# A memory-augmented attention kernel: the V projection of two steps in five passes, with the columns laid out by step pairs

## The chip, the cores and the metric

One NeuronCore of a Trainium2 chip. The metric is the device time of one execution in microseconds (us); lower is better. Each kernel was run a few times on the chip beside the kernel before. A run agrees with the next to about 0.3%.

## The reference, cut to what matters

The model has two layers. Each is an attention that walks over 64 segments of 32 tokens, carrying 8 memory rows from one segment to the next, followed by a gated feed-forward block. The width is 576, with 32 heads of 128 and a feed-forward width of 4608.

```python
for s in range(n_seg):                                  # 64 segments, strictly in order
    h = concatenate([mem, x[:, s*32:(s+1)*32]], axis=1)  # 8 memory rows + 32 tokens
    q, k, v = h @ Wq, h @ Wk, h @ Wv                     # 40 x 576 by 576 x (32 heads x 128)
    p = softmax(where(mask, q @ k.T * scale, -1e9))
    o = (p @ v) @ Wo
    mem = o[:, :8]                                       # the next segment needs this
    outs.append(o[:, 8:])
...
x = x + attention(layernorm(x)); x = x + silu_ffn(layernorm(x))   # twice
```

## The kernel before

The kernel runs 71 steps. In a step, layer 0 works on segment t and layer 1 on segment t − 7 (the constant `LAG`), so in 57 steps both layers are at work and their 40 columns share each matmul as 80 columns.

The order of TensorE's work is a fixed string of letters: a first part, a block of four steps repeated 11 times, and a last part. The letters that matter here are Q/q for the Q and K projections, S for scores, T for the transposes of the probabilities, P for probabilities times V, O/o for the output projection and its 64-row tail, X/x and V/v for the V projection of token and memory rows, F and W for the feed-forward block, and a, b, n, p for small transposes. "a" and "b" transpose the layer-normed rows of layer 0 and layer 1, four segments (a group) at a time; from there the rows are copied into `HT`, the transposed input of the projections. A small planner inside the kernel, with a cost for every instruction, decides in which order ScalarE and VectorE do the rest. Each engine then works through its own queue in that order.

The V projection of before takes three passes in a two-layer step: two for the token rows (two strips of 32 tokens for each of two quarters of the heads) and one for the memory rows, whose strip holds only 16 columns.

```python
POOLS = {"bank": 7, "y": 1, "qkt": 4, "vx": 2, "vm": 1, ..., "w2": 3, "htt": 4}

def v_mm(self, t, b, strips, tail):          # one pass: 4 column strips side by side
    for c in ((4,) if tail else range(4)):
        for r in (0, 1):
            for p0, c0, c1, q in strips:
                ...                          # 512 columns of Wv per matmul

def vx(self, t, k, b, tail):                 # tokens: k = 0, 1, so two passes
    todo = [(32*(2*ab + li), li, 2*k + ab) for ab in (0, 1) for li in (0, 1)]   # two layers
    ...
def vm(self, t, b, tail):                    # memory of both layers: one pass, 16 columns a strip
    return lambda n: self.v_mm(t, b, [(64*ab + 32*k, SEG, SEG + 2*MEM, 2*k + ab) ...], tail)
```

The layer norm's write into `HT` is one entry in one engine's queue for a whole group. Steps that lie side by side in `HT` are merged, so that it comes to 3 or 6 copies:

```python
def ln_nodes(tag, src, xn, deps, prio, wr, cost, wdeps):
    ...                                                   # stats, power, scaling on DVE and POOL
    d = node("PE", 5*0.056, em.ln_tr(xn, b[0]), ...)      # transposes into one PSUM bank
    return node("AD", cost, wr(b[0]), deps=[d], ...)      # one entry, on ScalarE or VectorE

def ht_write(self, li, g, b):
    ...                                                   # runs of neighbouring steps are merged
    for j0, s0, m in runs:
        self.cp(n, HT[:, s0:s0+m, 0:4, co:co+SEG], ps[:, 0:4, ...])     # m steps in one copy
        for r in (0, R64):
            self.cp(n, HT[r:r+R64, s0:s0+m, 4, co:co+SEG], ps[R64:P, 4, ...])
```

## Time and profile before

| | before |
|---|---|
| time, median of 3 | 2851.08 us (2850.7 to 2856.34) |
| TensorE busy | 98%, 62221 matmuls |
| VectorE, ScalarE, GpSimd busy | 75%, 38%, 2% |
| one block of four steps | 166.2 us |
| V projection | 7960 matmuls, 199 passes |

In the profile PE is TensorE, ACT is ScalarE, DVE is VectorE and POOL is GpSimd; L521 is a line of the kernel. All matmuls are issued from one helper line, all ScalarE copies from a second and all VectorE instructions from a third (L521, L524 and L527 here; L539, L542 and L545 in the changed kernel), so groups are told apart by the tiles they write and read. The prediction shows the page's lines.

### The profile page before, as it was taken

What the parts mean: (1) busy time and instruction counts of PE and PEld (TensorE: products, weight loads), DVE (VectorE), ACT (ScalarE), POOL (GpSimd) and SP (SyncE); (2) the same over time, 40 slices, a digit from 0 to 9 for tenths busy, and PEclk for the clock granted to TensorE, in tenths of its full rate; (3) what the DMA queues carried; (4) which work ended last, traced back from release to release, by engine and by line L of the source; (5) the groups of instructions that cost most, each with busy time, mean ns of one, the idle gap of its engine ahead of it and who ended that gap; (6) DMA issues with size and microseconds to landing.
All of it is one profiled execution on the core that took longest, in us unless ns stands there. A gap on an engine that the chain in (4) does not pass through costs nothing.

```text
span 2847.9 us, 137052 instructions
## 1 busy us (share of the span) xinstructions
PE 2784.7 (98%) x62221; PEld 2269.2 (80%) x62221; DVE 2129.7 (75%) x5300; ACT 1076.2 (38%) x2808; POOL 58.8 (2%) x110
## 2 busy tenths in 40 slices
PE   4999999999999999999999999999999999999998
PEld 3787887888888878888887888888788888788886
DVE  3677777777777787777778777777877777777776
ACT  1444343433434343343434334343333434343332
POOL 1000000000000000000000000000000000000000
PEclk9999999999999999999999999999999999999998
DMA  9063524234242433424243342424334242434467
GB/s 308 6 178 90 163 59 131 84 100 138 65 124 65 137 88 99 137 65 126 65 138 88 97 138 67 123 66 138 88 97 137 68 124 59 138 94 117 128 182 235
DMA packets 493416, 323.85 MB, mean 114 GB/s; under 512 B 26680, under 2 KB 488000, under 8 KB 492832
## 3 DMA queue, kind: packets, MB, share of 16 engines
q1 hardware_dynamic: 489808, 308.15, 36.9%
q8 instruction: 486, 7.96, 1.1%
q0 software_dynamic: 3024, 6.93, 0.8%
q14 instruction: 98, 0.80, 0.1%
HBM read 310.26 MB, written 2.36 MB: 110 GB/s over the span
## 4 chain that ended last, share of the span: by engine, by line
PE 92%; issue 4%; DMA 1%; DVE 1%; ACT 1%; SPq 0%; POOL 0%; DVEq 0%; ACTq 0%; POOLq 0%
PE bank L521 80%; PE YB L521 13%; DMA W<-in_A_Wk_dram 1%; DMA WV<-in_A_Wv_dram 0%; DVE HTT L527 0%; ACT HT L524 0%; DVE STAT L527 0%; DMA W2C<-in_B_w_dram 0%; DVE SME L527 0%; SPq L530 0%; DVE XR L527 0%; DVE QKT L527 0%; DVE PB L527 0%; ACT PTS L524 0%; DVE OT L527 0%
## 5 line engine op out<-in xcount | busy, mean ns | idle before, releaser
L521 PEld LDWEIGHTS <-W 128*128 128x128 bf16 (+1 forms) x29040 | 1212.5, 98 | 142.3 <-issue 56.4
L521 PE MATMUL bank<-HT,W 128*128 128x80 bf16 (+3 forms) x22720 | 821.5, 197 | 10.2 <-issue 5.7
L521 PE MATMUL bank<-XTB,W 128*128 128x256 bf16 (+3 forms) x6320 | 659.5, 262 | 0.1
L521 PE MATMUL bank<-WV,HT 128*32 128x512 bf16 (+3 forms) x7960 | 449.5, 382 | 18.6 <-DMA WV<-in_A_Wv_dram 18.2
L524 ACT ACTIVATE QKT<-bank 128x320 bf16<-128x320 f32 (+1 forms) x714 | 262.2, 409 | 487.0 <-PE bank L521 459.4
L521 PE MATMUL YB<-OT,WO 128*128 128x80 bf16 (+3 forms) x11360 | 434.8, 199 | 7.1 <-ACT HT L524 4.4
L521 PEld LDWEIGHTS <-WO 128*128 128x128 bf16 (+1 forms) x11400 | 389.7, 102 | 58.2 <-issue 43.7
L521 PEld LDWEIGHTS <-HT 128*32 128x32 bf16 (+3 forms) x7960 | 171.0, 92 | 215.6 <-issue 61.2
L527 DVE TENSOR_TENSOR PB<-SME,STAT 40x256 bf16<-40x256 f32 (+1 forms) x1024 | 321.4, 318 | 16.7
L521 PE MATMUL bank<-W2C,HTT 128*128 128x288 bf16 x2232 | 315.5, 287 | 1.8 <-DVE HTT L527 1.0
L527 DVE CAST QKT<-bank 128x320 bf16<-128x320 f32 (+1 forms) x422 | 183.8, 455 | 169.9 <-PE bank L521 167.4
L527 DVE TENSOR_REDUCE STAT<-SME 104x8 f32<-104x320 f32 (+1 forms) x568 | 272.4, 480 | 49.4 <-ACT SME L524 41.7
L527 DVE SCALAR_TENSOR_TENSOR XR<-bank,XR 128x288 f32<-128x288 f32 x576 | 247.3, 450 | 35.4 <-PE bank L521 23.8
L524 ACT ACTIVATE HTT<-bank 128x512 bf16<-128x512 f32 (+1 forms) x324 | 177.5, 549 | 237.6 <-PE bank L521 236.9
L521 PEld LDWEIGHTS <-HTT 128*128 128x128 bf16 x2304 | 209.1, 98 | 64.3 <-issue 11.0
L524 ACT ACTIVATE PTS<-bank 128x320 bf16<-128x320 f32 (+1 forms) x395 | 149.5, 408 | 208.0 <-PE bank L521 182.9
L527 DVE SCALAR_TENSOR_TENSOR HTT<-HTT,bank 128x512 bf16<-128x512 bf16 (+1 forms) x324 | 202.1, 624 | 33.1 <-ACT HTT L524 31.0
L524 ACT ACTIVATE SME<-SME 104x320 f32<-104x320 f32 (+1 forms) x284 | 133.1, 469 | 237.6 <-DVE SME L527 236.1
L527 DVE TENSOR_TENSOR HTT<-HTT,bank 128x512 bf16<-128x512 bf16 (+1 forms) x324 | 203.5, 628 | 22.1 <-PE bank L521 0.9
L524 ACT ACTIVATE OT<-bank 128x320 bf16<-128x320 f32 (+1 forms) x364 | 140.5, 406 | 185.1 <-PE bank L521 183.3
L527 DVE TENSOR_TENSOR SME<-bank,maskb 104x320 f32<-104x320 f32 (+1 forms) x284 | 137.4, 488 | 61.8 <-PE bank L521 57.9
L527 DVE CAST OT<-bank 128x320 bf16<-128x320 f32 (+1 forms) x204 | 94.3, 463 | 80.2 <-PE bank L521 77.3
(69 smaller groups left out, 1850.8 us busy)
## 6 DMA issues: line engine op xcount, KB each, us to landing
W<-in_B_w_dram SPq DMA_DIRECT2D x612, 256.0 KB, 3.5
W2C<-in_B_w_dram SPq DMA_DIRECT2D x306, 288.0 KB, 3.1
W<-in_B_w_dram SPq DMA_DIRECT2D x612, 32.0 KB, 3.0
W<-in_B_w_dram SPq DMA_DIRECT2D x10, 512.0 KB, 8.1
XR<-in_A_x_dram POOLq DMA_DIRECT2D x16, 288.0 KB, 2.8
WO<-in_A_Wo_dram SPq DMA_DIRECT2D x4, 1152.0 KB, 11.2
W<-in_A_Wq_dram SPq DMA_DIRECT2D x8, 512.0 KB, 8.2
W<-in_A_Wk_dram SPq DMA_DIRECT2D x8, 512.0 KB, 7.9
```

The costliest lines, as they stand in the source:

```text
L521: self.ch("PE", self.nc.tensor.matmul(out, lhsT=lhsT, rhs=rhs, start=start, stop=stop, skip_group_check=True, **k))
L524: self.ch("ACT", self.nc.scalar.activation(*a, **k))
L527: self.ch("DVE", getattr(self.nc.vector, fn_)(*a, **k))
```

## The change

Steps are taken in pairs. The second step of a pair leaves 16 of its 64 token rows out of the token passes, and they travel in the strips of its memory rows. Of a pair's 6 passes, 5 are left: two for tokens, one for the memory of the first step, two for the second step's memory with the 16 token rows. For that, `HT` is laid out as pairs of 160 columns, and the columns of the two layers are split and interleaved differently in the two steps. It follows that

- the copy out of the Q/K banks becomes two copies (256 and 64 columns),
- the write of a layer-norm group becomes four separate entries, one per step, each free to go to ScalarE or VectorE: 12 copies for layer 0 and, because layer 1's columns are split in two pieces, 24 for layer 1,
- the probabilities need zeros in new places, which GpSimd sets,
- the weight buffers of the second feed-forward matrix go from 3 to 2, and the V buffers become one pool of 4,
- the order string was searched anew.

```diff
-POOLS = {... "vx": 2, "vm": 1, ... "w2": 3, ...}
+POOLS = {... "v": 4, ... "w2": 2, ...}
+def role(t):
+    return (t - LAG) % 2

-        d = node("PE", 5 * 0.056, em.ln_tr(xn, b[0]), deps=[c] + list(wdeps), ...)
-        return node("AD", cost, wr(b[0]), deps=[d], prio=prio, rel=b, name=tag + "wr")
+        b = Slot("bank", users=len(writes))
+        d = node("PE", 5 * 0.056, em.ln_tr(xn, b), deps=[c], ...)
+        return [node("AD", cost, wr(b), deps=[d] + more, prio=prio, rel=[b], name=tag + "wr") for wr, cost, more in writes]

+X_AT = {(0, 0): [(0, 24, 32)], (0, 1): [(0, 104, 32)], (1, 0): [(0, 56, 24), (24, 0, 8)], (1, 1): [(8, 80, 24), (0, 152, 8)]}
-    def ht_write(self, li, g, b):
+    def ht_write(self, li, g, j, b):
...
-            for j0, s0, m in runs:
-                self.cp(n, self.T.HT[:, s0:s0 + m, 0:4, co:co + SEG], ...)
+            for x0, co, m in X_AT[self.kind(t, li), role(t)]:
+                x0 += j * SEG
+                self.cp(n, H_[:, 0:4, co:co + m], ps[:, 0:4, x0:x0 + m])
                 for r in (0, R64):
...
-    def vm(self, t, b, tail):
-        return lambda n: self.v_mm(t, b, [(64 * ab + 32 * k, SEG, SEG + 2 * MEM, 2 * k + ab) for ab in (0, 1) for k in (0, 1)], tail)
+    def vm(self, t, k, b, tail):
+        if role(t) == 0:
+            s = [(64 * ab + 32 * i, 0, 2 * i + ab) for ab in (0, 1) for i in (0, 1)]
+        else:
+            s = [(64 * ab + 32 * i, 96 + 32 * i, 2 * k + ab) for ab in (0, 1) for i in (0, 1)]
...
     def qk_ev(self, t, u, kind, q, b):
+                self.cp(n, dst[:, :, 0:64], src[:, :, 16:SW])
+                self.cp(n, dst[:, :, 64:SW], src[:, :, 0:16])
...
+            node("POOL", 1.2, em.pb_zero(pb), deps=[tr], prio=pf, rel=[pb], name="pbz")
```

## The prediction

> **What bounds the kernel now.** I read the page first (busy shares, slices, chain), then the waits of TensorE alone, then one stretch of time. The page of the kernel before:
>
> ```profile
> PE 2784.7 (98%) x62221; PEld 2269.2 (80%) x62221; DVE 2129.7 (75%) x5300; ACT 1076.2 (38%) x2808; POOL 58.8 (2%) x110
> ...
> PE   4999999999999999999999999999999999999998
> ...
> PE 92%; issue 4%; DMA 1%; DVE 1%; ACT 1%; SPq 0%; POOL 0%; DVEq 0%; ACTq 0%; POOLq 0%
> ...
> L521 PE MATMUL bank<-WV,HT 128*32 128x512 bf16 (+3 forms) x7960 | 449.5, 382 | 18.6 <-DMA WV<-in_A_Wv_dram 18.2
> ```
>
> TensorE is busy everywhere but in the first slice, and the chain that ended last is TensorE work for 92%. The last line is the V projection, which the change shortens: 7960 matmuls. A pass over it is 40 of them (32 on 128 rows, 8 on the 64-row tail), so 199 passes: 57 steps with both layers have 3 (two for tokens, one for memory), 14 steps with one layer have 2.
>
> The order of TensorE's blocks is fixed: a first part, a block of four steps repeated 11 times, a last part. The stretches of two repeats, and the waits of TensorE in the middle of the run:
>
> ```profile
> 655.92:822.12 166.20, 165.88 (x3576) 135.59 (x3577) 128.50 (x314) 63.27 (x156) 3.34 (x6) 1.00 0.35 102
> 822.12:988.33 166.21, 165.89 (x3576) 135.60 (x3577) 128.50 (x314) 63.78 (x159) 3.34 (x6) 1.00 0.35 102
> ```
>
> ```profile
> PE YB L521 <- ACT HT L524: 3.2, 10, 0.3
> ```
>
> Each repeat takes 166.2 us, TensorE is busy 165.9 of it (first pair of numbers), VectorE 128.5 and ScalarE 63.5, at full clock. In 1660 us TensorE waits for 3.2 us in all. So the four-step block is the sum of its matmuls and nothing else, and any pass removed from it should come off the end time.
>
> **What the Trainium skill says.** Perfetto Trace Analysis, section Identifying the Most-Contended Engine, warns that the busy share of matmuls is a bad measure of distance to the roofline because they are pipelined. The trace agrees: a V matmul is recorded with 382 ns, yet 32 of them take about 1.8 us. So I work with starts, not with durations. TensorE: Matmul & The Clock Gate, section Back-to-back issue gap, gives N/2.4 + 2.5 ns warm: 215.8 ns at 512 columns, 35.8 ns at 80. The trace agrees: QK blocks of 32 at 80 columns step 36 ns. TensorEngine Tiling (Array Packing), section Key Properties, says that changing the tiling mode drains the engine. In this trace a change costs about 0.10 us beyond the gap of the last matmul (median 131 to 134 ns from row mode to full mode, against 36). SBUF — State Buffer, section Who interferes with whom, says that a two-input VectorE instruction contends with GpSimd instructions that read SBUF, not with those that only write it; this matters for the new memsets, and no trace of before shows it.
>
> **The change, part by part.**
>
> Passes. Of each pair of two-layer steps, 6 passes become 5. 28 full pairs are concerned: counting the letters of the order gives 199 passes before and 171 after. Four matmuls run side by side in column tiles (eight in the tail), so a pass is 8 + 1 slots of 215.8 ns = 1.94 us. 28 x 1.94 = 54.4 us off, all on the bounding engine. The timeline shows a whole pass at 1512.84 us, the next block starting at 1515.02: 2.18 us, that is 1.94 plus two mode changes.
>
> Mode changes. Counting neighbours of different tiling mode in the two orders: 2217 before, 2115 after. 102 x 0.096 = 9.8 us off. For the four-step block it is 114 against 110, two passes fewer: 2 x 1.94 + 4 x 0.096 = 4.3 us. As a test of this book-keeping I summed the whole old block by measured gaps (32 QK of 32 x 36 ns, 16 WO, 12 V passes, 18 FFN ups of 16 x 109 ns, 18 downs of 8 x 122.5 ns, the small ones, 114 changes): 165.2 us, against 166.2 measured.
>
> Small terms. In 7 one-layer steps PV skips the token half: 112 row pairs of 25 ns, 2.8 us off. The step t = 64 is now handled as two-layered, 80 columns instead of 40 in QK, TR, PV and WO: some 500 slots of 11 ns, 5.5 us more. Together +2.7. All matmuls: 62221 - 1120 - 224 + 32 = 60909.
>
> Beside TensorE. Each QK eviction of a two-layer step becomes two copies, 256 and 64 columns. ScalarE takes 436 ns for 320 columns now, and instructions of those widths take 383 and 224, so about 0.17 us more for each of 928, of which the listing of the changed program puts 619 on ScalarE. HT is now written step by step, with 3 to 6 small copies of about 0.2 us each. 56 evictions of 512 columns (0.6 us) go. I expect ScalarE near 1300 us (46%) and VectorE near 2150 us (77%). Clearing PB moves to GpSimd: 284 memsets of 1024 elements; HT (2400 elements, 2093 ns) and YTS (1280, 1166 ns) give about 0.95 us each, so POOL rises from 59 to some 330 us. They only write, most VectorE instructions read PSUM or two inputs, and PB is double-buffered while its groups come about 10 us apart: off the path. W2 goes from 3 buffers to 2; from a pair of W2 blocks to the next I count at least 4.9 us of TensorE work, a load lands in 3.1.
>
> New waits. V passes are also filler that hides evictions. The new block ends TR, WO, PV, WO tail, WO, WO tail, then QK of the next step. Between the last PV and its WO lies one WO tail, 0.38 us with its changes. What is needed I take from 106.6 us of the trace: last PV at 106.59, WO at 107.16 after a 160-column eviction of 0.30, so 0.27 for the two handovers; with 320 columns 0.44 + 0.27 = 0.7. Wait: 0.3. After the last WO, QK needs the new memory columns; the same pattern at 254.25 us left TensorE idle for 0.34. Sum 0.7 us per block, where the old order had a V pass there: 11 x 0.7 = 7.7. The same count over the first and last parts gives 2 to 3 more, since V work of two steps now sits together. For copies longer than the order's search assumed I add 1. In all +11.
>
> Sum: 2851.1 - 54.4 - 9.8 + 2.7 + 11 = 2800.6, say 2801 us: 1.8% less. A block of four steps: 166.2 - 4.3 + 0.7 = 162.6 us.
>
> **The rivals.** (1) The order hides everything as the old one did (its waits were 3.2 us in 1660): then 2790 us, 2.1% less. For it: it was searched anew, so its author gave up fillers knowingly. Against it: the two short distances above. (2) Evictions become the limit: two copies in place of one, in queues whose order is fixed, delay the tanh and softmax work behind them, and banks come free later. For it: VectorE is already at 77% within a block. Against it: ScalarE has 60% to spare and takes two thirds of the copies; the shortest distance from a QK tail to its scores grows from 0.8 to 1.9 us. It would cost 1 to 2 us per block, giving 2810 to 2825. (3) Loads: with two W2 buffers a W2 load waiting in the queue holds up the W13 loads behind it. For it: the shortest distances, 4.9 us, leave 1 to 1.5 us. Against it: DMA is busy for 35%. It would show as waits on W2C or W, perhaps 0.5 us per block, 2807. (4) The passes are hidden anyway: excluded by 165.9 busy of 166.2.
>
> **Range and chances.** The removal is a count times a measured gap, good to some 3 us. The waits may be 0 or 25, so 2788 to 2818 should hold it 8 times in 10. The 2% line lies at 2794, below my value by about two thirds of the spread I give the waits: faster by over 2% 0.27, within 2% 0.72, slower 0.01.
>
> **What would show it.** Right: V matmuls 6840; repeats of 162 to 163 us; TensorE busy still over 98% inside them; short waits of TensorE for an OT eviction and for the HT write at the end of each fourth step; ScalarE near 46%, POOL near 12%. Wrong: a repeat at 162.0 or under (rival 1), waits of TensorE on QKT, PB, HTT or banks (rival 2), on W2C (rival 3), VectorE instructions longer than before while memsets run (contention), or a first stretch that ends later than before by more than a few us.

## More of the kernel before

One further stretch of before will be needed, because it shows a V pass at work as cover. The first fence is TensorE's timeline (start, duration, engine, line, operation, output<-inputs, forms, count, then in brackets the idle time ahead of it and who ended it), the second has lines of ScalarE and VectorE:

```profile
537.29 1.31 PE L521 MATMUL YB<-OT,WO 128*128 128x80 bf16 x32
538.53 2.25 PE L521 MATMUL bank<-WV,HT 128*32 128x512 bf16 x40
540.71 0.34 PE L521 MATMUL YB<-OT,WO 128*64 128x80 bf16 x8
```

```profile
537.19 1.71 ACT L524 ACTIVATE HT<-bank 128x256 bf16<-128x256 bf16 x6
538.93 0.23 ACT L524 ACTIVATE HT<-YB 128x64 bf16<-128x64 f32 x1
...
537.47 1.48 DVE L527 COPY HT<-bank 128x384 bf16<-128x384 bf16 x6
```

ScalarE writes a whole group of layer 0 into `HT` with 6 copies in 1.71 us, and then copies the new memory rows from the output bank `YB`. At the same time VectorE writes a whole group of layer 1 with 6 copies in 1.48 us. (Which is which follows from the widths: `HT` has 6 step slots here, so a group of layer 0 falls into runs of 4 or of 2 and 2 steps, one of layer 1 into 4, 3 and 1 or 1 and 3; 256 columns are two steps, 384 are three.) The two groups lie in two PSUM banks. TensorE spends the same time on the last output projection and on a V pass, and waits for nothing.

## The result, and the profile after

| | before | after | predicted |
|---|---|---|---|
| time, median of 4 | 2852.11 us (2850.7 to 2856.34) | 2842.86 us (2840.0 to 2844.68) | 2801 (2788 to 2818) |
| ratio after/before | | 0.9964, interval 0.9947 to 0.9981 | |
| block of four steps | 166.2 us | 165.3 (7 of 11), 165.8 to 165.9 (4 of 11) | 162.6 |
| matmuls; of the V projection | 62221; 7960 | 60909; 6840 | 60909; 6840 |
| VectorE, ScalarE, GpSimd busy, us | 2130, 1076, 59 | 2070, 1145, 328 | 2150, 1300, 330 |

A ratio is the mean time of one kernel's fast runs over that of the other's of the same rounds, so it is not quite the ratio of the medians quoted. The change saves 0.4%, which counts as the same time; the time lies 25 us above the range predicted.

From the page of the changed kernel (busy time and instructions of each engine; the chain that ended last; three groups of instructions with busy us, mean ns, idle time before and its releaser):

```profile
PE 2741.1 (97%) x60909; PEld 2257.2 (80%) x60909; DVE 2069.6 (73%) x5743; ACT 1144.9 (40%) x3629; POOL 328.4 (12%) x399
...
PE 92%; DVE 3%; ACT 2%; DMA 2%; issue 1%; SPq 0%; POOL 0%; DVEq 0%; ACTq 0%
...
L539 PE MATMUL bank<-WV,HT 128*32 128x512 bf16 (+1 forms) x6840 | 383.1, 384 | 7.8 <-DMA WV<-in_A_Wv_dram 7.7
L893 POOL MEMSET PB<- 128x1024 bf16 x284 | 270.0, 951 | 2117.9 <-PE bank L539 1837.0
L542 ACT ACTIVATE QKT<-bank 128x64 bf16<-128x64 f32 (+1 forms) x1371 | 316.6, 317 | 353.1 <-PE bank L539 347.8
```

The work went as planned. The passes are gone, and in the chain that ended last VectorE and ScalarE now have 5% between them instead of 2%. Next, two blocks of four steps (stretch, length, busy us and instructions of PE, PEld, DVE, ACT and POOL, then granted TensorE clock, DMA share, GB/s):

```profile
656.84:822.10 165.26, 162.39 (x3497) 133.93 (x3497) 123.04 (x341) 69.25 (x219) 18.54 (x22) 1.00 0.36 103
1437.38:1603.30 165.92, 163.69 (x3497) 135.10 (x3497) 123.16 (x342) 69.31 (x218) 18.54 (x22) 0.99 0.35 102
```

In a block of 165.26 us TensorE now stands still for 2.9 us, where it had been 0.3. The waits of TensorE between 740 and 2380 us, which is about ten blocks, name what it waits for (who waits <- for whom: us in all, times, the longest). In the kernel before, the same view has a single line, the one that the prediction shows.

```profile
PE YB L539 <- ACT HT L542: 9.7, 10, 1.0
PE bank L539 <- DVE XN L545: 6.7, 10, 0.7
PE bank L539 <- DVE YTS L545: 3.8, 6, 0.6
PE bank L539 <- ACT HT L542: 3.1, 9, 0.3
PE YB L539 <- ACT OT L542: 2.2, 9, 0.2
```

The last two lines are the two waits that the prediction foresaw at the end of each fourth step. The first three were not foreseen. They stand at the end of the third step of the block, where the order reads "…TWPOaOoobWQQqqp…". The order of before had "…OPWOooVvbWpQQqq…" there, with a V pass between the output tail and transpose b. One instance in TensorE's timeline:

```profile
1692.64 1.57 PE L539 MATMUL YB<-OT,WO 128*128 128x80 bf16 x40
...
1695.17 0.33 PE L539 MATMUL YB<-OT,WO 128*64 128x80 bf16 x8 [0.96 <-ACT HT L542]
...
1696.18 0.45 PE L539 MATMUL bank<-ident,XN 128*128 128x128 bf16 x5 [0.67 <-DVE XN L545]
...
1701.06 0.45 PE L539 MATMUL bank<-ident,YTS 128*128 128x128 bf16 x5 [0.63 <-DVE YTS L545]
```

The same time on ScalarE, and then on VectorE:

```profile
1692.84 0.69 ACT L542 ACTIVATE HT<-bank 128x128 bf16<-128x128 bf16 x3 [0.77 <-PE bank L539]
1694.19 0.69 ACT L542 ACTIVATE HT<-bank 128x128 bf16<-128x128 bf16 x3 [0.67 <-DVE HT L545]
1694.90 0.22 ACT L542 ACTIVATE HT<-YB 128x64 bf16<-128x64 f32 x1
```

```profile
1693.55 0.60 DVE L545 COPY HT<-bank 128x128 bf16<-128x128 bf16 x3 [1.02 <-ACT HT L542]
1694.91 0.60 DVE L545 COPY HT<-bank 128x128 bf16<-128x128 bf16 x3 [0.75 <-ACT HT L542]
1695.55 0.58 DVE L545 TENSOR_SCALAR XN<-XR,LNS 128x576 bf16<-128x576 f32 x1
1697.95 2.26 DVE L545 COPY HT<-bank 128x96 bf16<-128x96 bf16 x12 [1.43 <-ACT HT L542]
```

The four writes of layer 0's group never run side by side, although they write different steps. ScalarE makes three copies, VectorE waits for them and makes three, ScalarE waits for those, and so on. Behind ScalarE's second set stands the copy of the new memory rows (`HT<-YB`), for which the output projection's tail waits. Behind VectorE's second set stands the scaling (`XN`), for which transpose b waits. A little later the 12 copies of layer 1 stand in front of what transpose p needs (`YTS`).

What the four writes share is the PSUM bank that they read. The Trainium skill, page PSUM — Partial Sum Buffer, section PSUM bank collisions raise a hardware error, says that the compiler's scheduler adds a dependency between any two instructions on different engines that touch the same bank and the same 32-partition quadrant, reads included. The trace agrees: every bracket of an `HT` copy above, but that of the first set, names the other engine's `HT` copies. The tile that they write, `HT`, is not the reason: in the kernel before, the two engines wrote into it side by side at 537 us, from two banks. e3 below agrees, where two sets of copies from one bank write two different pairs of `HT` and still go one after the other (ScalarE's from 1677.72 to 1679.13 us, VectorE's from 1679.17, after a wait of 1.20 us for them). A run that gives each write a bank of its own was not made.

To see how much of the time this is, I summed over consecutive matmul starts what exceeds the expected gap (columns/2.4 + 2.5 ns, plus 0.097 us at a mode change), counting excesses over 25 ns. For the first, repeated and last part this gives 42.1 + 5.8 + 19.9 = 67.8 us before and 55.8 + 45.5 + 17.8 = 119.1 us after: 51 us more (some 10 us of it are matmuls that ran at half clock, of which the last section tells, though a block with one such stretch is only 0.5 us longer than one without). The work removed was to be 54.4 + 9.8 − 2.7 = 61.5 us. The difference is 10 us, and the spans of the two traces differ by 9.7 us (2847.9 and 2838.2).

The first part has the largest single case. The order there has "bOo|QQ" with no V pass in between:

```profile
534.26 1.57 PE L539 MATMUL YB<-OT,WO 128*128 128x80 bf16 x40
539.53 2.66 PE L539 MATMUL bank<-HT,W 128*128 128x80 bf16 x69 [3.70 <-ACT HT L542]
```

The same time on ScalarE, with one line of VectorE's:

```profile
534.46 1.22 ACT L542 ACTIVATE HT<-bank 128x96 bf16<-128x96 bf16 x6 [0.92 <-PE bank L539]
...
538.01 1.22 ACT L542 ACTIVATE HT<-bank 128x96 bf16<-128x96 bf16 x6 [2.33 <-DVE HT L545]
539.26 0.22 ACT L542 ACTIVATE HT<-YB 128x64 bf16<-128x64 f32 x1
...
535.72 2.26 DVE L545 COPY HT<-bank 128x96 bf16<-128x96 bf16 x12 [1.41 <-ACT HT L542]
```

Set this beside the stretch of before at 537 us. There a group of layer 1 was written in 1.48 us by one engine (VectorE), under cover of an output projection and a V pass. Now it takes from 534.46 to 539.23, 4.8 us, with 6 copies on ScalarE, 12 on VectorE and 6 on ScalarE, and TensorE stands still for 3.7 us of it. The copies themselves are 4.70 of these 4.8 us: the handovers cost next to nothing, but two engines are no faster than one. Over the whole run the copies from a layer-norm bank into `HT` went from 141 instructions to 558 (288 on ScalarE, 270 on VectorE), and from 40.5 us of engine time to 108.2.

### The profile page after: what moved, and what is told of

Read it like the earlier page. It is cut to its first block, busy times and chain, and to the rows that moved or that the text cites. A ratio compares the mean times of both kernels' runs of the same rounds, so it can differ in the third digit from the quotient of the medians.

```text
span 2838.2 us, 136886 instructions
## 1 busy us (share of the span) xinstructions
PE 2741.1 (97%) x60909; PEld 2257.2 (80%) x60909; DVE 2069.6 (73%) x5743; ACT 1144.9 (40%) x3629; POOL 328.4 (12%) x399
## 4 chain that ended last, share of the span: by engine, by line
PE 92%; DVE 3%; ACT 2%; DMA 2%; issue 1%; SPq 0%; POOL 0%; DVEq 0%; ACTq 0%
PE bank L539 80%; PE YB L539 12%; ACT HT L542 1%; DVE HT L545 1%; DMA W<-in_A_Wk_dram 1%; SPq L548 0%; DMA WO<-in_A_Wo_dram 0%; DVE XN L545 0%; DVE XR L545 0%; ACT OT L542 0%; DVE HTT L545 0%; DVE PB L545 0%; DVE STAT L545 0%; DVE LNS L545 0%; DVE SME L545 0%
## 5 line engine op out<-in xcount | busy, mean ns | idle before, releaser
L539 PEld LDWEIGHTS <-W 128*128 128x128 bf16 (+1 forms) x29040 | 1228.7, 99 | 156.6 <-issue 57.4
L893 POOL MEMSET PB<- 128x1024 bf16 x284 | 270.0, 951 | 2117.9 <-PE bank L539 1837.0
L542 ACT ACTIVATE QKT<-bank 128x64 bf16<-128x64 f32 (+1 forms) x1371 | 316.6, 317 | 353.1 <-PE bank L539 347.8
L539 PE MATMUL bank<-WV,HT 128*32 128x512 bf16 (+1 forms) x6840 | 383.1, 384 | 7.8 <-DMA WV<-in_A_Wv_dram 7.7
L545 DVE CAST QKT<-bank 128x64 bf16<-128x64 f32 (+2 forms) x693 | 186.4, 316 | 189.5 <-PE bank L539 186.4
L545 DVE TENSOR_TENSOR PB<-SME,STAT 40x128 bf16<-40x128 f32 (+1 forms) x1004 | 283.6, 321 | 15.5 <-DVE STAT L545 0.5
L539 PEld LDWEIGHTS <-HT 128*32 128x32 bf16 (+1 forms) x6840 | 149.6, 95 | 173.3 <-issue 44.2
L542 ACT ACTIVATE V<-bank 128x512 bf16<-128x512 f32 x256 | 141.8, 596 | 179.8 <-PE bank L539 177.7
```

The costliest lines, as they stand in the source:

```text
L539: self.ch("PE", self.nc.tensor.matmul(out, lhsT=lhsT, rhs=rhs, start=start, stop=stop, skip_group_check=True, **k))
L542: self.ch("ACT", self.nc.scalar.activation(*a, **k))
L545: self.ch("DVE", getattr(self.nc.vector, fn_)(*a, **k))
L893: return lambda n: self.ch("POOL", self.nc.gpsimd.memset(self.T.PB[:, pb.i], 0.0))
```

## The experiments

**Theory** (called A where the expectations abbreviate). The many small `HT` copies, strung into one chain over two in-order queues by their shared bank, delay the urgent work queued behind them. The planner does not know of the chain, so the order that was searched against its costs does not hold on the chip.

**Rivals.** The placing of the transposes in the order is at fault, and the number of copies is not. Or the taking of turns alone is at fault. Or the two-copy eviction of Q and K is (called B). Or the memsets on GpSimd are (called C). Or the V passes were not on the path, and their removal bought nothing (called D).

Unless said otherwise each experiment is one edit to the changed kernel, and gives the reference's result. All ratios are to the kernel before, from runs on the same chip (median of 2851.6 to 2853.1 us). Where an edit adds lines, the line numbers of the helpers shift by a few.

| edit | median us (range) | ratio (95%) | block of four, us |
|---|---|---|---|
| e1 transpose a earlier | 2841.73 (2840.33 to 2843.57) | 0.9968 (0.9951 to 0.9985) | 165.43 |
| e2 planner knows the chain | 2825.68 (2823.53 to 2826.01) | 0.9908 (0.9893 to 0.9923) | 164.68 |
| e3 one set of copies per pair | 2811.15 (2807.64 to 2813.05) | 0.9857 (0.9842 to 0.9872) | 163.79 |
| e4 = e1 + e3 | 2802.38 (2802.05 to 2806.52) | 0.9831 (0.9817 to 0.9846) | 163.15 |
| e5 Q/K in one copy | 2842.29 (2839.57 to 2845.43) | 0.9963 (0.9946 to 0.9979) | |
| e6 no memset | 2841.84 (2841.09 to 2843.06) | 0.9964 (0.9949 to 0.9979) | |
| e7 one V chunk twice | 2915.03 (2912.86 to 2916.2) | 1.0219 (1.0204 to 1.0234) | |
| e8 a group's writes on one engine | 2865.16 (2862.3 to 2867.97) | 1.0045 (1.003 to 1.006) | about 167.4 |
| e9 = e2 + e3 | 2807.47 (2806.08 to 2809.3) | 0.9841 (0.9826 to 0.9856) | 163.24 |
| e10 = e4 + transpose n later | 2802.19 (2799.74 to 2803.54) | 0.9821 (0.9806 to 0.9836) | 162.73 |
| e11 all of these | 2803.20 (2801.9 to 2803.67) | 0.9824 (0.9808 to 0.984) | 162.73 |
| e12 pair copies for layer 1 alone | 2823.71 (2822.48 to 2827.64) | 0.9904 (0.9887 to 0.992) | 164.43 |

### e1: transpose a moved away from the end of the step

```diff
-    "WFOfooQQqqQFfqFWWQ…POToTWPOaOoobWQQ…"
+    "WFOfooQQqqQFfqaFWWQ…POToTWPOOoobWQQ…"
```

> Only edit: in the repeated four-step block of the order the transpose of layer 0's next 128 rows (letter a) stands early in the third step instead of between its last two WO blocks. Same instructions, other queue order. Theory A (the step-by-step HT writes, 12 copies passed back and forth between ScalarE and VectorE, sit in front of the memory copy on ScalarE and of the LN scaling on VectorE at the end of the third step): the waits of 1.1 us (WO tail on the HT write) and 0.7 us (transpose on XN) per block go, a block falls from 165.3 to about 163.3 us, total near 2818 us. Rival B (the split QK evictions load the engines) and rival C (the memsets on GpSimd slow VectorE): no change, 2842 within 4.

Measured: 2841.73 us, no gain. Two lines of TensorE's waits between 740 and 2380 us; the first was not there before the edit, the second was 3.1 us:

```profile
PE bank L539 <- DVE HT L545: 12.7, 10, 1.3
PE bank L539 <- ACT HT L542: 5.3, 19, 0.3
```

The output tail's long wait is down from 9.7 to 3.2 us and that on `XN` is gone, as meant. In their place transpose p and the Q projection wait for layer 1's `HT` writes. Transpose p does not read `HT`, and in one instance its `YTS` was written by 1698.1 us, but it started at 1701.54, when VectorE's last copy of the group had ended. It probably waited for the PSUM bank that these copies still held, so a chain may delay TensorE in this way too; no run tests it. The expectation missed: moving one piece moved the wait and did not remove it. Against the first rival, the place alone is not the cause.

### e2: the planner is told that the writes of a group follow one another

```diff
-        return [node("AD", cost, wr(b), deps=[d] + more, ...) for wr, cost, more in writes]
+        out = []
+        for wr, cost, more in writes:
+            out.append(node("AD", cost, wr(b), deps=[d] + more + out[-1:], ...))
+        return out
```

> Only edit: the planner that orders the queues is told that the four HT writes of a group follow one another, as they do on the chip. Instructions are the same but for which of ScalarE and VectorE takes a copy. Theory A: the queues leave less waiting copies in front of urgent work, the waits at the end of the third step shrink by a part, total 2825 to 2838 us. Rivals B and C: 2842 within 4.

Measured: 2825.68 us, about 17 us faster than the changed kernel. No instruction was taken away; only the planner's picture became truer and its queues different. Beside the foreseen wait on `OT` (2.4 us) one line of waits is left in the middle part:

```profile
PE bank L542 <- ACT HT L545: 22.2, 30, 1.2
```

These are 24.6 us in all, hardly less than the changed kernel's 25.5. The gain shows in the starts of the matmuls: by the count of excess gaps above, done again, the first part falls from 56 to 49 us and the repeated one from 45 to 37. So the planner's blindness to the chain is part of the loss, and not all of it.

### e3: one set of copies for the two steps of a pair

```diff
-        for j in range(4):
-            out.append((... em.ht_write(li, g, j, b) ...))
+        for js in em.ht_parts(li, g):            # [0, 1], [2, 3], or single steps at an odd start
+            out.append((... em.ht_write(li, g, js, b) ...))
...
+            def two(at, step, xat, xstep, m):    # two pieces, `step` columns apart, in one copy
+                self.cp(n, strided(H_[:, 0:4], at, step, m), strided(ps[:, 0:4], x0 + xat, xstep, m))
+                for r in (0, R64):
+                    self.cp(n, strided(H_[r:r + R64, 4], at, step, m), strided(ps[R64:P, 4], x0 + xat, xstep, m))
+            if len(js) == 2 and self.kind(t, li) == 0:
+                two(24, 80, 0, SEG, SEG)
+            elif len(js) == 2:
+                two(56, 24, 0, 40, 24)
+                two(0, 152, 24, 8, 8)
```

> Only edit: the HT writes of the two steps of a pair are made by one set of copies, 12 instead of 24 small copies for layer 1 and 9 instead of 12 for layer 0, with the same values. Theory A: layer 1's writes (about 4.7 us of lockstep per group) halve, so the wait of 0.7 us for YTS and the waits of QK for HT behind it go, and part of the 1.1 us: a block near 164 us, total 2822 to 2832 us. Rivals B and C: 2842 within 4.

The copies of a group go from 24 to 12 for layer 1 and from 12 to 9 for layer 0, with the same bytes in the same places. Measured: 2811.15 us, 32 us faster than the changed kernel and 11 below the range expected. The waits on `XN` and `YTS` are gone from the middle part. The wait of the output tail stays, because 9 copies of layer 0 are still in front of it:

```profile
PE YB L541 <- ACT HT L544: 10.7, 10, 1.1
```

This is the largest gain of a single edit. The edit also makes fewer turns of a group (two for layer 1, three for layer 0, where there were four); e8 below takes the turns away and keeps the copies, and gains nothing, so the number of copies is what remains.

### e4: fewer copies and transpose a earlier

> Both edits of the first and third experiment together. Theory A: only the waits that the prediction had named remain (0.3 us before the last WO and 0.4 us before QK at the end of the fourth step), a block near 162.6 us, half-clock windows gone, total 2805 to 2815 us. Rivals B and C: 2842 within 4.

Measured: 2802.38 us, 40 us faster than the changed kernel and 3 below the range expected; the block is 163.15 us. The edit of e1, which bought nothing by itself, is worth 9 us once the copies are few.

```profile
PE bank L541 <- ACT HT L544: 3.4, 10, 0.3
PE YB L541 <- ACT HT L544: 3.2, 10, 0.3
PE YB L541 <- ACT OT L544: 2.4, 10, 0.2
PE bank L541 <- DVE HT L547: 2.3, 10, 0.2
```

All that is left are short waits, two of which the prediction had foreseen. The sum of excess gaps is 44.6 + 20.2 + 16.2 = 81.0 us, 13 us more than before. With 61.5 us of work removed that gives 48 us, and the span of its trace is 2800.3 against 2847.9: 47.6 us less.

### e5: Q and K leave the bank in one copy (values wrong)

```diff
-            elif role(t) == 0:
-                self.cp(n, dst[:, :, 0:64], src[:, :, 16:SW])
-                self.cp(n, dst[:, :, 64:SW], src[:, :, 0:16])
             else:
-                ...
+                self.cp(n, dst[:, :, 0:SW], src[:, :, 0:SW])
```

> Wrong results on purpose: the QK eviction of a two-layer step is one copy of 320 columns instead of two of 256 and 64, as before the change; everything else stays, the queue orders nearly so. Theory A: the evictions are off the path, 2842 within 5 us. Rival B: the splits are what was lost, total 2810 to 2825 us.

Measured: 2842.29 us, unchanged. (The columns are in the wrong places. The comparison with the reference still passed, since attention has a small share in the output; the result is wrong all the same.) ScalarE's group:

```profile
L542 ACT ACTIVATE QKT<-bank 128x320 bf16<-128x320 f32 (+1 forms) x752 | 277.4, 415 | 365.9 <-PE bank L539 362.6
```

In the changed kernel the group has 1371 instructions and 316.6 us. The 619 extra copies cost 39.2 us, 63 ns each, and none of it reaches the end. The rival of the two-copy eviction falls.

### e6: no memset (values wrong)

```diff
-            tr = node("PE", 8 * mm80, em.ptr(t, g, pb, bt), ..., acq=[pts] + bt, name="TR")
-            node("POOL", 1.2, em.pb_zero(pb), deps=[tr], prio=pf, rel=[pb], name="pbz")
+            tr = node("PE", 8 * mm80, em.ptr(t, g, pb, bt), ..., acq=[pts] + bt, rel=[pb], name="TR")
```

> Wrong results on purpose: the 284 memsets that clear PB on GpSimd are left out, so POOL falls from 328 to about 58 us. Theory A: 2842 within 3 us, VectorE durations unchanged. Rival C (memsets hold up VectorE or PB): clearly faster, by 10 us or more, and shorter VectorE instructions.

Measured: 2841.84 us, unchanged, with GpSimd down to 2% and VectorE as it was:

```profile
PE 2745.0 (97%) x60909; PEld 2260.7 (80%) x60909; DVE 2069.3 (73%) x5743; ACT 1145.4 (40%) x3629; POOL 59.3 (2%) x115
```

Neither the memsets' own time nor contention by them is the cause. Single VectorE instructions agree: the subtraction `SME<-SME,STAT` on two inputs takes 492 ns before, 492 after and 492 without memsets.

### e7: one chunk of every V pass done twice (the second overwrites the first, so the values stay right)

```diff
-        for c in ((4,) if tail else range(4)):
+        for c in ((4,) if tail else (0, 0, 1, 2, 3)):
```

> Right results: the first of the four chunks of every V pass is computed twice, the second overwriting the first: 171 x 8 more matmuls, 2 slots of 215.8 ns a pass. If V passes lie on the path as the prediction says, 171 x 0.432 = 73.8 us more, about 2916 us, minus what it fills of waits (few of these lie behind a V pass). Rival D (the passes lay beside other work, so that taking 28 away saved little): far less than half of this.

Measured: 2915.03 us, about 73 us slower than the changed kernel.

```profile
L539 PE MATMUL bank<-WV,HT 128*32 128x512 bf16 (+1 forms) x8208 | 457.2, 383 | 7.6 <-DMA WV<-in_A_Wv_dram 7.5
```

There are 8208 − 6840 = 1368 more matmuls, four side by side, so 342 slots, which at 215.8 ns is 73.8 us. V work is on the path at its full price. The rival that the removed passes bought nothing falls, and the prediction's −54.4 us was sound.

### e8: all writes of a group on one engine

```diff
+        cost = tuple(sum(c[i] for _, c, _ in writes) for i in (0, 1))
+        n = node("AD", cost, lambda n: [wr(b)(n) for wr, _, _ in writes], deps=[d] + ..., rel=[b], name=tag + "wr")
+        return [n] * len(writes)
```

> Only edit: all HT writes of a group go to one engine, as one unit for the planner, so no copy waits for the other engine. Theory A, back and forth as the main part of it: faster, 2825 to 2835 us. If instead the number of copies in front of urgent work is what counts, no better than 2842, since one queue then holds 2.8 us (layer 0) or 4.7 us (layer 1) of copies at once.

Measured: 2865.16 us, 0.5% slower than the kernel before and 0.8% slower than the changed one. There is no turn-taking any more, but up to 24 copies (4.98 us of ScalarE's time at 1541.43 us) now stand in front of everything else in one queue:

```profile
PE bank L543 <- DVE YTS L549: 18.5, 9, 2.1
PE bank L543 <- ACT HT L546: 16.6, 20, 1.3
```

So the turn-taking alone is not the cause, against what one could read from the brackets in the timelines. It fits that what counts is how many copies stand in a queue ahead of urgent work. (The edit also makes a group's write wait for the readers of all four of its steps at once, and the clock was at half for one window in ten of the eleven blocks instead of four, so not all of the 23 us need come from the queue.)

### e9: fewer copies, and the planner knows the chain

> The edits of the second and third experiment together: fewer copies, and the planner knows that they follow one another. If the two act on the same loss (copies in front of urgent work), the gains of 17 and 30 us do not add: 2795 to 2808 us, block 163 to 163.5 us. If each acted on a loss of its own they would add to about 2795.

Measured: 2807.47 us. Alone the edits gained about 17 and 32 us; together they gain 35. They remove largely the same loss.

### e10: as e4, with the feed-forward transpose n one place later

```diff
-    "…TOPoxTOPonTOPoOo"
+    "…TOPoxTOPoTOPonOo"
```

> The fourth experiment, and in the repeated block the letter n (transposes for the FFN, 0.28 us) moved from ahead of the last TR to between the last PV and its WO. The prediction's step on filler: the wait of 0.31 us of the last WO for the OT eviction goes, that of QK for the memory columns (0.41 us) stays: block 162.85 us, 11 x 0.3 = 3 us less than the fourth experiment, about 2799 us. If the wait at the block's end were not a matter of filler, no change, 2802.

Measured: the block went to 162.73 us as expected, and the wait on the `OT` eviction is gone from the list; the other three lines of e4 are there unchanged.

The total of 2802.19 us is no better than e4's, however. The two ran on different chips; against the kernel before, the ratios are 0.9821 and 0.9831 with intervals of 0.0015 to either side, so a gain of 3 us and none cannot be told apart. In the two traces e10's first part ended at 563.2 us and e4's at 559.7, which takes back most of the 4.6 us that the blocks gained. The start-up loads are a likely place, which no run here isolates.

### e11: everything together

> All edits together: fewer copies, the planner's knowledge, the early transpose of layer 0, the later n. Expected the fastest: block about 162.6 us, first and last parts 3 to 6 us shorter than in the fourth experiment, total 2790 to 2798 us, so about 2% below the kernel before.

Measured: 2803.20 us, a miss. The repeated block is as short as in e10, but the first and last parts did not shrink. Their excess gaps, 46.1 and 20.2 us, are no smaller than e4's 44.6 and 16.2.

### e12: pair copies for layer 1 alone

```diff
-            if out and role(t) == 1:
+            if li and out and role(t) == 1:
```

> The third experiment for layer 1 alone (12 copies instead of 24 per group); layer 0 keeps its 12 copies in four turns. If layer 1's copies cause the wait for YTS and the long wait of QK for HT, and layer 0's the wait of the WO tail and of the transpose for XN: the first two go, the last two (1.1 and 0.7 us per block) stay; block near 164.4 us, total 2820 to 2828 us. If layer 1 is all of it: 2811 as in the third experiment; if layer 0 is all of it: 2842.

Measured: 2823.71 us. The waits on `YTS` are gone. The output tail's and `XN`'s, which stand behind layer 0's copies, are unchanged from the changed kernel:

```profile
PE YB L541 <- ACT HT L544: 9.7, 10, 1.0
PE bank L541 <- DVE XN L547: 6.7, 10, 0.7
```

Merging layer 1's copies thus gains 19 us, and merging layer 0's as well brings e3's further 13. Each of these waits goes with the copies that stand ahead of it.

**The best versions.** e4, e10 and e11, at 2802 to 2803 us, beat both kernels: 1.7 to 1.8% below the kernel before and some 40 us below the changed one. Neither is clear of 2%.

## Why the prediction was wrong

- **The bound, and the price of the passes: right.** The kernel is TensorE's matmuls end to end, and e7 shows V work on the path at 215.8 ns a slot. The counts of matmuls came out exactly.
- **The mode changes and small terms: consistent.** They were not tested alone, but with 61.5 us removed, the measured waits account for the spans of the changed kernel and of e4 against before to within 1 us.
- **The waits: the step that failed.** The prediction booked the writes under "Beside TensorE": "HT is now written step by step, with 3 to 6 small copies of about 0.2 us each." It gave them no place in the sum, and closed with "In all +11." That term measured +51 us, matmuls at half clock included. The size of one copy was right (0.19 us on average), and the number per step too. What was left out is that four such writes per group share one bank and so run one after another, that they stand in the same queues as the memory copy, `XN` and `YTS`, and that the new order has no V pass left where one had covered such a write. e3, e4 and e12 show it: with fewer copies and one letter moved, the term measures +13 and the time is 2802.4 us against the predicted 2801. That this is so close is in part luck: of the +13 the repeated part has +14 where 7.7 was predicted, the first +2.5, and the last part is 4 us shorter.
- **The two named waits: right.** They are in the profile at 0.2 and 0.3 us a block, where 0.3 and 0.34 were worked out.
- **The rivals.** Rival 2 had the right kind of cause, queues that delay the work behind them, but sought it in the Q/K evictions. e5 shows those to be free. Its case "against", that ScalarE has 60% to spare, was no protection: a mean share says nothing about the order within a queue. Rival 3, the weight loads, does not appear: the middle part of the changed kernel shows no wait on `W2C`.
- **Side estimates.** ScalarE rose by 69 us and not by some 220. Splitting a copy costs 63 ns and not 170, which is some 66 us of the difference; the rest was not traced. VectorE fell by 60 us where a rise of 20 was predicted. The memset, estimated at 0.95 us from the larger ones, measured 0.951.
- **A small remainder.** In four blocks the clock was granted at half for one window (last section), which costs some 0.5 us each. They seem to follow from the waits (not shown): e1, where these lie further apart, has no such window in its blocks.

What stays open is whether e10 and e11 turn their shorter blocks into a shorter total, what a bank for each write would do, how much of the loss lies in the new order itself (the two orders were never exchanged), and how much a new search against true costs would still bring.

## What to carry to other kernels

When a change on a saturated engine takes work away, ask what that work had been covering, and check in the queues of the other engines what will stand in front of the next urgent instruction. A layout that multiplies small copies out of one PSUM bank is to be booked as one serial chain, in number of copies times duration, and not as a busy share. Here merging copies with a strided access took most of the loss away, while moving one piece only moved the wait. If the order of work comes from a cost model, put such a chain into the model: here the corrected planner alone, with the order as it was, brought 17 us (e2).

## What the Trainium skill lacked or had wrong

- **TensorE: Matmul & The Clock Gate, section What's actually happening:** it gives half clock after at least one idle window of about 3.4 us (elsewhere it names frequent short idles, without a share). Here the clock was halved though TensorE was not idle for such a window. In the changed kernel, the stretch ahead of a halved one and the halved one itself (columns as for the blocks above):

```profile
1527.50:1530.90 3.40, 1.76 (x42) 1.46 (x39) 2.07 (x9) 1.36 (x8) 0.00 (x0) 1.00 0.00 0
1530.90:1534.30 3.40, 3.40 (x37) 2.80 (x35) 1.97 (x12) 1.61 (x8) 0.00 (x0) 0.50 0.28 77
```

  TensorE had been busy for 1.76 us of 3.40 (52%), with several short waits, and the next 3.40 us ran at a clock of 0.50. The same happened at 1199.8, 1862.0 and 2193.1 us. No threshold comes out of it: the 3.40 us from 537.6 (busy for 1.47 us) and those from 701.4 (1.76 us) were followed by full clock.
- **PSUM — Partial Sum Buffer, section PSUM bank collisions raise a hardware error:** the added dependency is stated; what it does to a group of small copies dealt to two engines is not. Here 24 copies out of one bank took 4.8 us in turns on two engines and 4.98 us on one (e8), against 1.48 us for 6 copies on one engine.
- **TensorEngine Tiling (Array Packing), section Key Properties:** no figure for the drain at a change of tiling mode; here about 0.10 us each.
